# A second MLP in two passes, with both of its products made of seven block products

## The chip, the cores and the metric

The kernel runs on one core of a Trainium2 chip, with all five engines of that core: TensorE (PE) for matmuls, VectorE (DVE), ScalarE (ACT) and GpSimd (POOL) for the rest, SyncE (SP) for most DMAs. The metric is the time of one execution on the device, in microseconds.

## The reference

All is float32. Three parts follow one another on 4 batches of 576 tokens and 512 features:

```python
x  = attention(q, k, v)                    # 8 heads of 64; half local, half strided masks
u  = x + real(fft(fft(x, axis=1), axis=2)) # 4 x 576 x 512
x  = u + relu(norm(u) @ w_ch1) @ w_ch2     # first MLP, 512 -> 2048 -> 512
h  = relu(x.T @ w_tok1) @ w_tok2           # token mixing, 576 -> 256 -> 576
u  = x + h.T
out = u + relu(u @ w_ch1b) @ w_ch2b        # second MLP, 512 -> 1536 -> 512
```

Each float32 operand of a product is kept as a high and a low part in a format that PE takes, and a product is three matmuls: high by high, high by low, low by high.

## The kernel before

PE's work lies in this order: attention with the Fourier part, the first MLP (class Mlp, L381 and L399, six chunks of 384 tokens by 16 blocks f of hidden features), the token mixing (c1 at L704, c2 at L724, batch by batch), and the second MLP. A scheduler sets the order of the instructions on each engine from the order of the program and its dependencies; tile pools decide when a buffer may be written again.

The second MLP takes 9 chunks of 256 tokens. A chunk has 6 steps m. In each, gemm1 makes two blocks of h, for features f = m + 6 and m, with 24 matmuls of 256 columns (L777); ACT takes them out of PSUM with the relu (L783, L784), DVE forms four sums of 128-column blocks (L789) and the low parts (L791, L792), ACT the high part of the sums (L790); gemm2 multiplies 2 by 2 blocks of h by 2 by 2 blocks of w2b with seven block products in place of eight, each of three matmuls of 256 columns, 21 matmuls a step (L807). At a chunk's end eleven additions on DVE (L831) combine the seven products into the result, which is stored.

The seven combinations of w2b are made ahead: blocks() is called 12 times, at f % 4 == 1 of the first MLP's chunks 2 to 4. It loads raw weights in double precision, turns them into float32 on ACT and DVE (L92 to L97), adds blocks on POOL (L120), splits them into high and low on ACT and POOL (L123, L124), and SP stores them to DRAM (wsd). POOL's queue loads them again in 42 DMAs (L619). The 12 blocks of w1b are converted in the last chunk of the first MLP (load_wb). Results of the token mixing go to DRAM (u2d, L735), come back in tiles of 128 tokens (u_load, L753) and are transposed on PE (L762).

## Time and profile before

| | us |
|---|---|
| three runs | 950.62, 954.13, 953.64 (median 953.64) |
| span of the profiled execution | 947.8 |
| between the span and the median | 5.8 |
| PE busy in the span | 919.9 (97%) |
| DVE, ACT, POOL busy | 538.8, 374.1, 205.2 |

The profile gives one execution's span, from the first to the last instruction; no other time of that execution is given, and the runs are timed from outside. A busy time counts a matmul up to its modelled end, so that matmuls overlap: the distance between the starts of two of them is what PE needs for one. Idle time of an engine that nobody waits for costs nothing.

### The profile page before, as it was taken

Reading aid. Unit: us, or ns where it says so; the run is one execution under the profiler, and the core shown is the slowest. Engines: PE = TensorE matmul, PEld = TensorE weight load, DVE = VectorE, ACT = ScalarE, POOL = GpSimd, SP = SyncE. Lnnn points to the kernel's source line nnn. Section 1 sums busy time; section 2 is a strip of 40 time slices with the busy share of each in tenths; the row PEclk is TensorE's granted clock in tenths of the full one; section 3 lists DMA queues with packets and bytes.
Section 4 is the critical chain, followed back from the end, with each engine's and each line's share of the span. In section 5 each row is a group of like instructions: output and inputs, shape, how many; then the busy total and the mean of one; then the engine's idle time right before and its main releaser. Section 6 shows DMA issues by size and latency. Waiting matters only on the chain.

```text
span 947.8 us, 16036 instructions
## 1 busy us (share of the span) xinstructions
PE 919.9 (97%) x6094; PEld 850.5 (90%) x6094; DVE 538.8 (57%) x1182; ACT 374.1 (39%) x998; POOL 205.2 (22%) x230
## 2 busy tenths in 40 slices
PE   6979999999999999999999999999999999999997
PEld 5969998899888888999999988779999999999997
DVE  4659987898975544321213678444545545553554
ACT  5969776444433334121112445212333333333332
POOL 4213203233344354000000666342000000000000
PEclk9979999999999999999999999999999999999999
DMA  9988862344436767200100445598011101100000
GB/s 261 275 273 258 264 199 88 105 157 142 152 105 212 235 187 206 90 1 1 67 1 5 150 147 161 159 288 269 12 34 45 42 5 46 46 24 22 24 24 23
DMA packets 73286, 113.85 MB, mean 120 GB/s; under 512 B 6803, under 2 KB 39417, under 8 KB 73209
## 3 DMA queue, kind: packets, MB, share of 16 engines
q1 hardware_dynamic: 65192, 99.09, 33.4%
q0 software_dynamic: 7760, 13.52, 5.0%
q8 instruction: 48, 0.79, 0.4%
q10 hardware_dynamic: 256, 0.21, 0.1%
q14 instruction: 30, 0.24, 0.1%
HBM read 78.97 MB, written 33.82 MB: 119 GB/s over the span
## 4 chain that ended last, share of the span: by engine, by line
PE 71%; DVE 9%; DMA 7%; issue 5%; ACT 3%; POOL 3%; SPq 1%; DVEq 0%; POOLq 0%; ACTq 0%
PE h L777 16%; PE oo L807 14%; PE oo L399 12%; PE h L381 12%; PE tk L704 3%; PE tu L724 3%; PE sc L180 2%; DMA wraw<-in_w2a_dram 2%; PE av L222 2%; DVE wu L96 2%; DMA wraw<-in_w2b_dram 1%; DVE wu L97 1%; PE g L302 1%; DVE wu L94 1%; DMA wsd<-wbl 1%
## 5 line engine op out<-in xcount | busy, mean ns | idle before, releaser
L807 PE MATMUL oo<-w2b,hh 128*128 128x256 f32 x756 | 140.4, 284 | 0.0
L381 PE MATMUL h<-uth,wAh 128*128 128x384 f32 x384 | 130.2, 340 | 0.0
L381 PE MATMUL h<-utl,wAh 128*128 128x384 f32 x384 | 129.6, 337 | 0.0
L381 PE MATMUL h<-uth,wAl 128*128 128x384 f32 x384 | 129.5, 337 | 0.0
L777 PE MATMUL h<-uth,w1bl 128*128 128x256 f32 x432 | 120.9, 280 | 0.0
L777 PE MATMUL h<-utl,w1bh 128*128 128x256 f32 x432 | 120.8, 280 | 0.0
L386 DVE SCALAR_TENSOR_TENSOR hl<-h,hh 128x384 fp32r<-128x384 f32 x96 | 53.1, 553 | 119.0 <-ACT hh L385 119.0
L777 PE MATMUL h<-uth,w1bh 128*128 128x256 f32 x432 | 120.7, 280 | 0.0
L399 PE MATMUL oo<-wAh,hh 128*128 128x512 f32 x288 | 114.5, 399 | 2.9 <-ACT hh L385 1.6
L807 PEld LDWEIGHTS oo<-w2b,hh 128*128 128x128 f32 x756 | 116.2, 189 | 0.0
L399 PE MATMUL oo<-wAl,hh 128*128 128x512 f32 x288 | 113.6, 395 | 0.0
L399 PE MATMUL oo<-wAh,hl 128*128 128x512 f32 x288 | 106.1, 397 | 1.4 <-DVE hl L386 1.3
L807 PE MATMUL oo<-w2b,hl 128*128 128x256 f32 x378 | 104.4, 282 | 0.0
L385 ACT ACTIVATE hh<-h 128x384 fp32r<-128x384 f32 x96 | 46.1, 483 | 118.1 <-PE h L381 117.9
L789 DVE TENSOR_TENSOR hz<-hw 128x128 f32<-128x128 f32 x108 | 26.6, 287 | 114.0 <-ACT hw L783 114.0
L783 ACT ACTIVATE hw<-h 128x512 f32<-128x512 f32 x54 | 32.3, 599 | 148.4 <-PE h L777 148.4
L777 PEld LDWEIGHTS h<-uth,w1bh 128*128 128x128 f32 x432 | 81.3, 188 | 0.2
L777 PEld LDWEIGHTS h<-uth,w1bl 128*128 128x128 f32 x432 | 81.2, 188 | 0.1
L777 PEld LDWEIGHTS h<-utl,w1bh 128*128 128x128 f32 x432 | 81.2, 188 | 0.1
L381 PEld LDWEIGHTS h<-uth,wAl 128*128 128x128 f32 x384 | 72.2, 188 | 3.0
L381 PEld LDWEIGHTS h<-utl,wAh 128*128 128x128 f32 x384 | 72.2, 188 | 2.9
L381 PEld LDWEIGHTS h<-uth,wAh 128*128 128x128 f32 x384 | 72.1, 188 | 2.0
(166 smaller groups left out, 1866.1 us busy)
## 6 DMA issues: line engine op xcount, KB each, us to landing
w2b<-wsd POOLq DMA_DIRECT2D x42, 256.0 KB, 5.3
wraw<-in_w1a_dram SPq DMA_DIRECT2D x16, 512.0 KB
wraw<-in_w2a_dram SPq DMA_DIRECT2D x16, 512.0 KB
wraw<-in_w2b_dram SPq DMA_DIRECT2D x48, 128.0 KB
wraw<-in_w1b_dram SPq DMA_DIRECT2D x12, 512.0 KB
wsd<-wbh SPq DMA_DIRECT2D x12, 448.0 KB
wsd<-wbl SPq DMA_DIRECT2D x12, 448.0 KB
out_dram<-u SPq DMA_DIRECT2D x16, 256.0 KB
```

The costliest lines, as they stand in the source:

```text
L96: v.scalar_tensor_tensor(out=u, in0=high, scalar=-2**31, in1=u, op0=ALU.bitwise_and, op1=ALU.bitwise_or)
L180: last = nc.tensor.matmul(out=sc[:q, j * k:(j + 1) * k], lhsT=qz[self.g][:, e, hp, qs], rhs=k_t[self.b, self.g][:, hp, ks], start=False, s ...
L381: nc.tensor.matmul(out=h[:, :384], lhsT=l[:, ws], rhs=r[:, kd, :], start=x == 0, stop=x == 11)
L385: nc.scalar.activation(out=hh, in_=h[:, :384], func=AF.Relu)
L386: nc.vector.scalar_tensor_tensor(out=hl, in0=h[:, :384], scalar=0.0, in1=f32(hh), op0=ALU.max, op1=ALU.subtract)
L399: nc.tensor.matmul(out=self.o[c][i], lhsT=l[:, s], rhs=r, start=first and x == 0, stop=last and x == 2)
L704: nc.tensor.matmul(out=hp[m], lhsT=wt1(w, t, m)[q], rhs=r[q], start=t == 0 and x == 0, stop=t == 4 and x == 2)
L724: nc.tensor.matmul(out=o[:q0 + n], lhsT=wt2(w, k, 128 * t - q0, q0 + n), rhs=r, start=k == 0 and x == 0, stop=k == 1 and x == 2)
L777: nc.tensor.matmul(out=h[:, 256 * i:256 * i + 256], lhsT=l[:, ws], rhs=r[:, kd, 0:256], start=x == 0, stop=x == 11)
L783: nc.scalar.activation(out=w, in_=h, func=AF.Relu)
L789: nc.vector.tensor_tensor(out=o, in0=x, in1=y, op=op)
L807: ends.append(nc.tensor.matmul(out=acc[c][bank][:, 256 * half:256 * half + 256], lhsT=lh[:, s], rhs=r, start=m == 0 and x == 0 and half == ...
```

## The change

The first product of the second MLP is now made of seven block products as well, and the second MLP goes in two passes. Tokens are taken in three superchunks of 768. u_stage loads and transposes six tiles of a superchunk; u_ops forms the block sums and splits the seven operands. A Unit is one step m of a superchunk: seven products, each of six matmuls of 384 columns (L821). The sums build up in three PSUM banks z, y and w; ACT copies z at three points (snap), DVE adds the copies into h (into), and relu stands at the end (ACT for one block, DVE for three). Units go in pairs, their products interleaved by hand (double). The h of the first two superchunks goes to DRAM (hd) and is loaded again; that of the last stays in SBUF.

The second pass has its order written out by hand: 54 steps of 21 matmuls of 256 columns, as before, over 9 groups G of 256 tokens. In it h is loaded six steps ahead and split three steps ahead (h_split: the four sums now on POOL, two copies on ACT, two subtractions on DVE), and finish() combines the products; for the last group bank by bank. blocks() is called 24 times, for w1b too, and load_wb's conversions of w1b are gone. All block operands are loaded on SP's queue (load_ops). The low parts of the token mixing's input for batches 2 and 3 move from DVE to POOL.

```diff
...
-NP2, NC2 = NF2 // 2, 9
+NP2, NS = NF2 // 2, 3
...
-    def blocks(m, c0):
...
+    def blocks(w, m, c0):
+        src = a["w" + w + "b"]
+        order = ((0, 256), (0, 0), (1, 0), (1, 256)) if w == "2" else ((1, 0), (0, 0), (0, 256), (1, 256))
...
-        for o, x, y in ((t1, b12, b11), (t2, b22, t1), (t3, b22, b12), (t4, t2, b21)):
-            nc.gpsimd.tensor_tensor(out=o, in0=x, in1=y, op=ALU.subtract)
...
+        for o, x, y, plus in sums:
+            nc.gpsimd.tensor_tensor(out=o, in0=x, in1=y, op=ALU.add if plus else ALU.subtract)
...
-            nc.sync.dma_start(out=wsd[m][:, :, o:o + 128].rearrange("b p c -> p b c"),
+            nc.sync.dma_start(out=wsd[w][m][:, :, o:o + 128].rearrange("b p c -> p b c"),
...
-            elif len(w1b) < NF2:
-                f = len(w1b)
-                pool, tag = (wa, "wa") if f < 2 else (wb, "wb") if f < 10 else (wc, "wc")
-                w1b.append(slot_w(a["w1b"][f], pool, tag, "w1b"))
-
-        def load_w2(ms):
...
-                    nc.gpsimd.dma_start(out=t, in_=wsd[m][x])
...
+        def load_ops(w, m):
+            wo[w, m] = []
...
+                nc.sync.dma_start(out=f32(t), in_=wsd[w][m][x])
+                wo[w, m].append(t)
...
-                nc.vector.tensor_tensor(out=l[q], in0=r[q], in1=f32(h[q]), op=ALU.subtract)
+                (nc.gpsimd if b > 1 else nc.vector).tensor_tensor(out=l[q], in0=r[q], in1=f32(h[q]), op=ALU.subtract)
...
-                blocks(m, 128 * h)
+                blocks("2", m, 128 * h)
+            if 2 <= c < NCH - 1 and f % 4 == 3:
+                m, h = divmod((c - 2) * 4 + f // 4, 2)
+                blocks("1", m, 128 * h)
...
-                if b == 0 and t < 3:
-                    u2[t] = r
-                else:
-                    nc.sync.dma_start(out=u2d[p][j, q, :], in_=r[q])
+                nc.sync.dma_start(out=u2d[p][j, q, :], in_=r[q])
...
-        def gemm1(c, m):
...
+        def u_stage(s):
+            q = [ga.tile([P, 4, 384], F32, tag=nm, name=nm, bufs=1) for nm in ("qa", "qb")]
...
+                for half in range(2):
+                    u = u_load(6 * s + 3 * half + i)
+                    tp = ps_m("ut")
+                    for kd in range(4):
+                        nc.tensor.transpose(tp[:, kd * P:(kd + 1) * P], u[:, kd * P:(kd + 1) * P], ident)
+                    nc.scalar.activation(out=q[half][:, :, i * P:(i + 1) * P],
+                                         in_=tp.rearrange("p (k t) -> p k t", k=4), func=AF.Copy)
+            return q
+
+        def u_ops(s, q):
+            qa, qb = q
...
+            eng = nc.vector if s == 0 else nc.gpsimd
+            for o, x, y, e in ((t1, b12, b11, eng), (t2, b22, t1, eng), (b12, b22, b12, nc.gpsimd), (t4, b21, t2, nc.gpsimd)):
+                e.tensor_tensor(out=o, in0=x, in1=y, op=ALU.subtract)
+            src = dict(b11=b11, b21=b21, t2=t2, t1=t1, t3=b12, t4=t4, b22=b22)
+            U[s] = {}
+            for nm in UB:
+                t = gp.tile([P, 12, P], F32R, tag=nm, name="u" + nm, bufs=1)
+                h, l = (t[:, c:c + 6].rearrange("p (k g) t -> p k (g t)", k=2) for c in (0, 6))
+                nc.scalar.activation(out=h, in_=src[nm], func=AF.Copy)
+                e = nc.gpsimd if s == 0 and nm in ("t3", "b22") else nc.vector
+                e.tensor_tensor(out=l, in0=src[nm], in1=f32(h), op=ALU.subtract)
+                U[s][nm] = h, l
...
+            def product(self, n, bank, first):
+                i, nm = PRODUCTS[n]
+                w = wo["1", self.m][i]
+                h, l = U[self.s][nm]
                 x = 0
-                for kd in range(4):
-                    ws = slice(kd * P, (kd + 1) * P)
-                    for l, r in ((wh, th), (wh, tl), (wl, th)):
-                        nc.tensor.matmul(out=h[:, 256 * i:256 * i + 256], lhsT=l[:, ws], rhs=r[:, kd, 0:256],
-                                         start=x == 0, stop=x == 11)
+                for kd in range(2):
+                    for c, r in ((0, h), (0, l), (256, h)):
+                        Unit.last = nc.tensor.matmul(out=bank[:, :384], lhsT=w[:, c + kd * P:c + kd * P + P], rhs=r[:, kd],
+                                         start=first and x == 0, stop=x == 5,
+                                         skip_group_check=True)
...
+            def snap(self):
+                t = wa.tile([P, 512], F32, tag="wa", name="snap")[:, :384]
+                nc.scalar.activation(out=t, in_=self.z[:, :384], func=AF.Copy)
+                return t
...
+            def into(self, i, bank, t):
+                for o, x, y in self.pieces(i, bank, t):
+                    nc.vector.tensor_tensor(out=o, in0=x, in1=y, op=ALU.add)
+
+            def step(self, n):
+                if n == 1:
+                    self.z = ps_h("z")
+                    self.product(1, self.z, True)
+                    self.q1 = self.snap()
+                elif n == 2:
+                    w = ps_o("w")
+                    self.product(2, w, True)
+                    self.into(2, w, self.q1)
+                elif n == 6:
+                    self.product(6, self.z, False)
+                    self.u1 = self.snap()
+                elif n == 5:
+                    self.y = ps_o("y")
+                    self.product(5, self.y, True)
+                    if self.u2 is not None:
+                        self.into(1, self.y, self.u2)
+                elif n == 7:
+                    self.product(7, self.z, False)
+                    self.u2 = self.snap()
+                    if self.y is not None:
+                        self.into(1, self.y, self.u2)
+                elif n == 4:
+                    self.product(4, self.z, False)
+                    for o, x in self.pieces(0, self.z):
+                        nc.scalar.activation(out=o, in_=x, func=AF.Relu)
+                elif n == 3:
+                    self.product(3, self.y, False)
+                    self.into(3, self.y, self.u1)
+
+            def store(self):
+                for p in self.parts:
+                    nc.vector.tensor_scalar_max(p[:, :, 1:4], p[:, :, 1:4], 0.0)
+                    if self.s < NS - 1:
+                        nc.sync.dma_start(out=hd[self.s][self.m], in_=p.rearrange("p g i t -> p (g i t)"))
+
+        def double(s, m, then={}):
+            a, b = Unit(s, m), Unit(s, m + 1)
+            for x, n in ((a, 1), (b, 1), (a, 2), (b, 2), (a, 6), (b, 6), (a, 5), (a, 7), (b, 7), (b, 5),
+                         (a, 3), (b, 3), (a, 4), (b, 4)):
+                x.step(n)
+                if x is a and n == 4:
+                    a.store()
+                if x is b and n in then:
+                    h_split(*then[n])
+            b.store()
...
         c_load(3, range(5))
-        for b in range(2, 4):
-            hs.append(c1(b))
-        for T in range(2):
-            transposes(T)
-        for b in range(2, 4):
-            c2(b, hs[b])
-        load_w2(range(1, NP2))
-
...
-        steps = [(c, m) for c in range(NC2) for m in range(NP2)]
-        for i, (c, m) in enumerate(steps):
-            gemm1(c, m)
-            if c + 1 < NC2:
...
+        hs.append(c1(2))
+        load_ops("1", 0)
+        c2(2, hs[2])
+        q = u_stage(0)
+        load_ops("1", 1)
+        u_ops(0, q)
+        hs.append(c1(3))
+        c2(3, hs[3])
+        for m in range(2, NP2):
+            load_ops("1", m)
...
+        Gs = [3 * NS - 3, 3 * NS - 2, 3 * NS - 1] + list(range(3 * NS - 3))
+        steps = [(G, m) for h in ((0, 4), (4, NP2)) for G in Gs[:2] for m in range(*h)]
+        steps += [(G, m) for G in Gs[2:] for m in range(NP2)]
...
+        def h_load(G, m):
+            s, g = divmod(G, 3)
+            if s < NS - 1:
+                if m % 3 == 0:
+                    h_load.t = ha.tile([P, 3, 4, P], F32, tag="hs", name="hw", bufs=3)
+                w = rows[G, m] = h_load.t[:, m % 3]
+                nc.sync.dma_start(out=w, in_=hd[s][m][:, 512 * g:512 * g + 512].rearrange("p (i t) -> p i t", i=4))
...
+        def h_split(G, m):
+            w = rows.pop((G, m))
+            z = wa.tile([P, 4, P], F32, tag="wa", name="hz")
+            a12, a22, a11, a21 = (w[:, i] for i in range(4))
+            s1, s2, s3, s4 = (z[:, i] for i in range(4))
+            t = gp.tile([P, 12, P], F32R, tag=UB[steps.index((G, m)) % NP2], name="ht", bufs=1)
+            wh, wl, zh = (t[:, c:c + n] for c, n in ((0, 3), (3, 3), (6, 4)))
+            zl = wa.tile([P, 4, P], F32R, tag="wa", name="zl")
+            nc.scalar.activation(out=wh, in_=w[:, 0:3], func=AF.Copy)
+            for o, x, y, op in ((s1, a21, a22, ALU.add), (s2, s1, a11, ALU.subtract), (s3, a11, a21, ALU.subtract),
+                                (s4, a12, s2, ALU.subtract)):
+                nc.gpsimd.tensor_tensor(out=o, in0=x, in1=y, op=op)
+            nc.vector.tensor_tensor(out=wl, in0=w[:, 0:3], in1=f32(wh), op=ALU.subtract)
+            nc.scalar.activation(out=zh, in_=z, func=AF.Copy)
+            nc.vector.tensor_tensor(out=zl, in0=z, in1=f32(zh), op=ALU.subtract)
+            ops[G, m] = wh, wl, zh, zl
+
+        for s in range(NS):
+            if s + 1 == NS:
+                gast.close()
+                ha = hst.enter_context(tc.tile_pool(name="ha", bufs=1, side="left", reuse_waits="tile"))
+            for m in range(0, NP2, 2):
+                double(s, m, {2: steps[0], 6: steps[1], 5: steps[2]} if s + 1 == NS and m == NP2 - 2 else {})
+                if m == 0 and s + 1 < NS:
+                    q = u_stage(s + 1)
+                if s + 1 == NS:
+                    load_ops("2", m)
+                    load_ops("2", m + 1)
+            if s + 1 < NS:
+                u_ops(s + 1, q)
+
+        BANKS = ((0, 0, "w", 2, 0), (0, 1, "z", 1, 4), (1, 0, "z", 2, 5), (1, 1, "z", 0, 3), (2, 0, "w", 0, 1),
...
+
+            def fourth():
+                v(c21, c21, o[3][:, 0:256], ALU.subtract)
...
+            if G != Gs[-1]:
+                gemm2(G, [NP2 - 1], BANKS)
+            for bank, part in enumerate((first, second, third, fourth)):
+                if G == Gs[-1]:
+                    gemm2(G, [NP2 - 2, NP2 - 1], BANKS[2 * bank:2 * bank + 2])
+                part()
+            acc.pop(G)
+            return store
...
+        ahead, split, later, us2 = 6, 3, {}, {}
+        with tc.manual_schedule():
+            for x, (G, m) in enumerate(steps):
                 if m == 0:
-                    for T in (2 * c + 2, 2 * c + 3):
-                        if T > 2:
-                            u_load(T)
-                if m in (2, 3):
-                    transposes(2 * c + m)
-            if i:
-                gemm2(*steps[i - 1])
-        gemm2(*steps[-1])
+                    acc[G] = [(ps_o if Gs.index(G) % 2 else ps_h)("oo") for _ in range(3)] + [ps_m("oo")]
+                    us2[G] = u_load(6 * (G // 3) + G % 3), u_load(6 * (G // 3) + G % 3 + 3)
+                if x in later:
+                    later.pop(x)()
+                if x + ahead < len(steps):
+                    h_load(*steps[x + ahead])
+                if x + split < len(steps):
+                    h_split(*steps[x + split])
+                if m == NP2 - 1:
+                    later[x + 3] = finish(G)
+                elif G != Gs[-1] or m < NP2 - 2:
+                    gemm2(G, [m], BANKS)
+            for x in later:
+                later[x]()
```

Up to the first new block sums, in chunk 2 of the first MLP, the instructions stand in the same order in both kernels. Three places behind that show what is moved.

PE where the second MLP begins, before (tu: token mixing, h: the first product) and then after (ut: transposes, z: a first-product bank):

```order
L724 MATMUL tu<-uth,wth 128x512
L724 MATMUL tu<-utl,wth 128x512
L724 MATMUL tu<-uth,wtl 128x512
L777 MATMUL h<-uth,w1bh 128x256 x2
L777 MATMUL h<-utl,w1bh 128x256
L777 MATMUL h<-uth,w1bl 128x256
L777 MATMUL h<-uth,w1bh 128x256
L777 MATMUL h<-utl,w1bh 128x256
```

```order
L732 MATMUL tu<-hl,wth 128x512
L732 MATMUL tu<-hh,wtl 128x512
L732 MATMUL tu<-hl,wth 128x512
L732 MATMUL tu<-hh,wtl 128x512
L821 MATMUL z<-ub_6645,wo 128x384 x12
L732 MATMUL tu<-hh,wth 128x512 x3
L769 MATMUL ut<-ident_r,u 128x128 x4
L732 MATMUL tu<-hl,wth 128x512
```

Before, the first product starts between the last batch's matmuls with 256 columns; now products of 384 columns stand between matmuls of the mixing, in sixes and twelves.

SP in the same place, before and then after (wo: the block operands; cr and x2d: inputs of the mixing; u2d: its results; u: tiles loaded for the transposes):

```order
L653 DMA cr<-x2d_78 128x512 x3
L735 DMA u2d_79<-u 128x512
L735 DMA u2d_79<-u 64x512
L753 DMA u<-u2d_79 128x512
L735 DMA u2d_79<-cr 128x512 x3
L653 DMA cr<-x2d_78 64x512
L735 DMA u2d_79<-cr 128x512
L735 DMA u2d_79<-cr 64x512
L753 DMA u<-u2d_79 128x512 x2
```

```order
L622 DMA wo<-wsd_84 128x512
L740 DMA u2d_79<-u 128x512 x3
L756 DMA u<-u2d_79 128x512
L622 DMA wo<-wsd_82 128x512 x5
L740 DMA u2d_79<-u 128x512
L740 DMA u2d_79<-u 64x512
L622 DMA wo<-wsd_83 128x512
L756 DMA u<-u2d_79 128x512
L740 DMA u2d_79<-cr 128x512
L756 DMA u<-u2d_79 128x512
L622 DMA wo<-wsd_83 128x512 x2
L740 DMA u2d_79<-cr 128x512 x2
```

Before, SP had only the mixing's loads and stores and the tiles here, since POOL's queue loaded the block operands; now the operands stand between stores and tiles in one queue.

DVE in the second MLP's steps before, then DVE after (ht and zl: low parts; lm and u: combining the products), then POOL after (hz: sums of blocks of h):

```order
L792 TENSOR_TENSOR hl<-hz,hh 128x512
L789 TENSOR_TENSOR hz<-hw 128x128 x2
L789 TENSOR_TENSOR hz<-hz,hw 128x128
L791 TENSOR_TENSOR hl<-hw,hh 128x384
L789 TENSOR_TENSOR hz<-hw,hz 128x128
L766 TENSOR_TENSOR utl<-ut,uth 128x4x128
```

```order
L929 TENSOR_TENSOR ht<-hw,ht 128x384
L931 TENSOR_TENSOR zl<-hz,ht 128x512
L973 TENSOR_TENSOR lm<-oo,lm 128x256 x2
L973 TENSOR_TENSOR u<-oo,u 128x256 x2
L973 TENSOR_TENSOR u<-u,lm 128x512
L973 TENSOR_TENSOR u<-oo,u 128x512
L973 TENSOR_TENSOR u<-u,lm 128x512
L973 TENSOR_TENSOR u<-u,oo 128x256
L929 TENSOR_TENSOR ht<-hw,ht 128x384
L931 TENSOR_TENSOR zl<-hz,ht 128x512
```

```order
L928 TENSOR_TENSOR hz<-hw 128x128
L928 TENSOR_TENSOR hz<-hw,hz 128x128
L928 TENSOR_TENSOR hz<-hw 128x128
L928 TENSOR_TENSOR hz<-hz,hw 128x128
L928 TENSOR_TENSOR hz<-hw 128x128
```

The four additions of 128 columns have left DVE, where they stood between the low parts, and POOL, which had none in this stage, has them one after another.

## Rows read from the trace of the kernel before

**Rows 1.** The page, part 2: tenths of busy time in 40 slices.

```profile
PE   6979999999999999999999999999999999999997
...
PEclk9979999999999999999999999999999999999999
```

**Rows 2.** Stretches: length, busy time of each engine (instructions), granted clock, DMA share, GB/s.

```profile
250.00:400.00 150.00, 147.40 (x732) 129.67 (x732) 85.86 (x161) 51.24 (x100) 59.98 (x80) 1.00 0.57 174
...
600.00:650.00 50.00, 50.00 (x226) 37.88 (x225) 21.26 (x32) 7.61 (x14) 20.28 (x36) 1.00 0.83 255
650.00:941.00 291.00, 291.00 (x2464) 290.99 (x2462) 150.37 (x431) 96.89 (x186) 1.33 (x3) 1.00 0.11 35
941.00:948.00 7.00, 0.20 (x2) 0.00 (x0) 3.06 (x9) 0.00 (x0) 0.00 (x0) 0.79 0.19 75
```

**Rows 3.** Groups of instructions from 640 us on: busy us, mean ns, idle before.

```profile
L807 PE MATMUL oo<-w2b,hh 128*128 128x256 f32 x756 | 140.4, 284 | 0.0
L777 PE MATMUL h<-uth,w1bl 128*128 128x256 f32 x432 | 120.9, 280 | 0.0
...
L792 DVE TENSOR_TENSOR hl<-hz,hh 128x512 fp32r<-128x512 f32 x54 | 37.3, 691 | 26.2 <-ACT hh L790 26.1
...
L791 DVE TENSOR_TENSOR hl<-hw,hh 128x384 fp32r<-128x384 f32 x54 | 29.7, 550 | 0.0
```

**Rows 4.** Timeline of PE, second MLP: start us, us, engine, line and operation.

```profile
699.74 0.28 PE L777 MATMUL h<-uth,w1bl 128*128 128x256 f32 x1
...
701.50 0.28 PE L777 MATMUL h<-uth,w1bl 128*128 128x256 f32 x1
```

**Rows 5.** Timeline of PE, first MLP, products of 384 columns.

```profile
420.87 0.34 PE L381 MATMUL h<-uth,wAh 128*128 128x384 f32 x1
...
423.35 0.34 PE L381 MATMUL h<-uth,wAl 128*128 128x384 f32 x1
```

**Rows 6.** The chain of waits at the end: start us, us, what.

```profile
930.85 2.52 PE oo L807 x21
...
936.19 3.47 PE oo L807 x29
...
943.76 0.34 DVE u L831
```

**Rows 7.** Timeline of SP at the end.

```profile
943.79 0.81 SPq L834 DMA_DIRECT2D out_dram<-u  x2
```

**Rows 8.** Timeline of SP: raw loads of the first and the fourth of four block sets.

```profile
334.87 2.08 SPq L88 DMA_DIRECT2D wraw<-in_w2b_dram  x4
...
358.17 1.77 SPq L88 DMA_DIRECT2D wraw<-in_w2b_dram  x4
```

**Rows 9.** Groups of POOL over the whole span.

```profile
L120 POOL TENSOR_TENSOR wt<-wu 128x128 f32<-128x128 f32 x24 | 10.6, 462 | 39.8 <-DVE wu L97 39.8
```

**Rows 10.** Timelines of POOL and DVE near 270 us and 543 us, where both work.

```profile
270.17 0.69 DVE L96 SCALAR_TENSOR_TENSOR wu<-wraw,wu 128x512 int32<-128x512 int32 x1
270.90 1.67 DVE L97 SCALAR_TENSOR_TENSOR wu<-wraw,wu 128x512 int32<-128x512 int32 x1
...
270.54 1.47 POOL L103 TENSOR_TENSOR wAl<-wu,wAh 128x512 fp32r<-128x512 f32 x1 [3.25 <-ACT wAh L102]
...
543.71 1.33 POOL L103 TENSOR_TENSOR w1bl<-wu,w1bh 128x512 fp32r<-128x512 f32 x1 [1.94 <-ACT w1bh L102]
...
543.82 1.78 DVE L96 SCALAR_TENSOR_TENSOR wu<-wraw,wu 128x512 int32<-128x512 int32 x1
```

**Rows 11.** Timeline of POOL: additions of 128 columns back to back.

```profile
289.33 0.88 POOL L120 TENSOR_TENSOR wt<-wu 128x128 f32<-128x128 f32 x2 [4.36 <-DVE wu L97]
290.17 0.46 POOL L120 TENSOR_TENSOR wt<-wu,wt 128x128 f32<-128x128 f32 x1
```

**Rows 12.** Stretches around a long wait of PE, columns as in rows 2.

```profile
57.00:64.00 7.00, 0.29 (x3) 0.15 (x2) 4.18 (x13) 1.88 (x7) 1.59 (x2) 0.79 1.00 344
64.00:71.00 7.00, 6.95 (x31) 6.18 (x32) 4.96 (x11) 6.04 (x26) 1.47 (x2) 0.50 0.90 273
```

More of the change, by code (lines that the diff above doesn't have):

```diff
@@ new lines, in u_load @@
+            u = lp.tile([P, DM], F32, tag="u", name="u", bufs=6)
+            nc.sync.dma_start(out=u, in_=u2d[T // 9][T % 9])
+            return u
+        U = {}
+        UB = ("b11", "b21", "t2", "t1", "t3", "t4", "b22")
+        def u_stage(s):
+            q = [ga.tile([P, 4, 384], F32, tag=nm, name=nm, bufs=1) for nm in ("qa", "qb")]
+            for i in range(3):
+                for half in range(2):
[6 more added lines that the diff above has]
+            return q
@@ L867, in attention_fourier_mlp_kernel @@
+        gst.close()
+        hst.close()
         wcst.close()
```

216 lines of the change are left out of this document (115 added, 101 removed).

## The prediction

> **What bounds the kernel now.** I read four views, in this order: the slices, the stretches, the groups of instructions, and last the chain of waits. The slices show PE at 9 from the fifth slice to the last but one, at the granted clock's upper level nearly throughout [rows 1]. The stretches make that sharp: from 650 to 941 us PE is busy 291.0 of 291.0 us and DVE 150.4, with POOL at 1.3 and the DMA share at 0.11 [rows 2]. So the second MLP is bound by the number of matmul columns on PE; DVE has half its time free, POOL all of it. The chain ends in the same way: PE alone up to 939.66 us, then some 4 us of DVE, then the stores [rows 6]. Hence I price first what the change takes off PE, and after that everything that could stop PE from running without gaps.
>
> **The change part by part.**
>
> *First product of the second MLP.* Before: 3 x 432 = 1,296 matmuls of 256 columns at L777 [rows 3]. One issues every (701.50 - 699.74)/15 = 0.1173 us [rows 4]: the group's 280 ns is the time of one in the pipeline, not its price. Sum 152.0 us. After: 3 superchunks x 6 steps x 7 products x 6 matmuls = 756 of 384 columns at L821. The first MLP has such matmuls, one every (423.35 - 420.87)/14 = 0.1771 us [rows 5], sum 133.9 us. Difference: **-18.1 us**. It is all on the path, as PE has no gap there. The second product keeps its 1,134 matmuls of 256 columns, and the transposes stay 72.
>
> *Tail.* Before, the last matmul ends near 941.1 and the span at 947.8 us: 6.7 us for the additions at L831, of which the last ends at 944.1, and stores issued at 943.79 [rows 6, 7]; the second issue ends at 944.60, 3.2 us before the end. After, the last tile's banks are added one by one while PE still works, so behind the last matmul stand one addition of 256 columns, one issue and the landing: 0.4 + 0.4 + 3.2 = 4.0, and I allow 0.3 for hand-overs. **-2.4 us**, bounds -3 and +1 (the copies of the banks, on ACT, come late).
>
> *Twelve more sets of block sums.* Twelve sets for w1b join twelve for w2b during chunks 2 to 4 of the first MLP. A set's loads come every (358.17 - 334.87)/3 = 7.8 us [rows 8], so 24 sets take some 187 us from 261 on, to about 450, well before the token mixing, which holds the stretch from 600 on [rows 2]. ACT and DVE serve PE between them; the stretch that held the twelve lost PE 150 - 147.4 = 2.6 us [rows 2]. As many again would be +2.6; what the twelve conversions of w1b that go had cost is not counted. I take **+1.5**, bounds 0 and 6 (twice the loss seen, and the first sets delay one another).
>
> *Into the second MLP.* All tiles now make the round trip through DRAM, six are transposed, and DVE and POOL form seven operands for 768 tokens before the first product; SP's queue carries 42 operand loads between them, which were POOL's. Queued behind a waiting SP load are the u2d stores and the next batch's loads, and for those PE waits. The cover is the token mixing of the last two batches, whose matmuls stand between the products in PE's new order. That cover shares the DMA engines with the loads: 0.83 busy at 255 GB/s in that stretch [rows 2], and 14 operand loads of 256 KB are needed for the first pair, 3.7 MB or 14 us at that rate. I follow the chain by hand through the order and find 0 to 2 us of slack at two operands. Estimate **+3**, bounds 0 and 10.
>
> *Between the products.* Sums build up in three kinds of PSUM bank with copies between; the tight place is product 3, which waits for an addition (0.55 us for 384 columns [rows 3]) behind product 5 with one product of the other step, 6 x 0.1771 = 1.06 us, between. That fits unless DVE is in another instruction. There are nine pairs and three starts of a superchunk: **+2**, bounds 0 and 9 (a microsecond in each pair).
>
> *Second product: POOL beside DVE.* This is the term with the widest bounds. Each of 54 steps is 21 matmuls, 2.52 us of PE [rows 6], and needs four additions of 128 columns, now on POOL, and two subtractions (384 and 512 columns) on DVE, all with two inputs in SBUF. The trace of before shows that such instructions do not run together. A DVE instruction of 512 columns that took 0.69 us alone took 1.67 and 1.78 beside a POOL instruction, each ending 0.56 us after POOL's end (272.57 against 272.01; 545.60 against 545.04). And where DVE was first, POOL's 512 columns took 1.47 us and ended 1.15 after DVE's end (272.01 against 270.86) [rows 10]. So one shuts the other out for most of its time: 0.56 of 0.69 on DVE, about 0.13 less than its duration, and on POOL about 0.15 less than an undisturbed one. For POOL's 128 columns at 0.462 [rows 9] that leaves 0.31; for DVE's 384 columns at 0.55 [rows 3], 0.42.
>
> Per step, the exclusive part is 4 x 0.31 + 0.56 + 0.42, and a sixth of two 512-column additions of each finished tile, 0.19: 2.41 us, below the 2.52 of PE. But POOL's own starts are 0.42 apart ((290.17 - 289.33)/2 [rows 11]), and a DVE instruction that slips in holds it up for its exclusive part less the 0.11 that is free anyway: 4 x 0.42 + 1.17 - 2.33 x 0.11 = 2.59 us per step. The lower bound of the cost is nothing (2.41 fits). If nothing slips into POOL's gaps, a step is 1.68 + 1.17 = 2.85 us and the cost 0.33 x 51 = 17 us; at the far end, with whole durations one after another, it is 4 x 0.462 + 0.55 + 0.69 + 2 x 0.69 / 6 = 3.32 us, and 0.80 x 51 = 41 us. I take POOL's 2.59, as rows 10 and 11 are nearest to it: (2.59 - 2.52) x 51 = 3.6, and with the waits of the first steps **+5**.
>
> The Trainium skill has a rule for this, in "SBUF — State Buffer", section "Who interferes with whom": a DVE instruction with two SBUF inputs contends with a POOL instruction that reads SBUF, and whichever was first has the ports for its whole instruction. Rows 10 agree on the blocking and show a shorter hold. Taken at its word it speaks against the change, by the far end above; by the rows it costs 5.
>
> *Round trip of h.* Twelve stores of 768 KB in 90 us of products, and 36 loads of 256 KB over as many steps, beside a DMA share of 0.11 [rows 2]: covered, issued six steps ahead. If a load were late, PE would wait once, not in every step.
>
> **The sum.** The profiled execution has a span of 947.8 us; the median of the runs is 953.64, so 5.8 lie outside the span, by the median, and I leave them as they are. 953.6 - 18.1 - 2.4 + 1.5 + 3 + 2 + 5 = **944.6**, I say 945.
>
> **The rivals.**
>
> A. *The port decides the second product, and the change loses.* POOL and DVE exclude each other, and neither slips into the other's gaps. For it: rows 10, and that PE can't start a step without both engines' results. Against: the exclusive parts add to 2.41, and POOL may run three steps ahead. The point from which it makes the kernel slower than before is a step of 2.52 + (5 + 9)/51 = 2.79 us, since my forecast with its 5 has 9 in hand. At 2.85 the time is 939.6 + 17 = 957, at whole durations 939.6 + 41 = 981. I give it 957 to 981, mostly the lower half.
>
> B. *A long wait at the entry.* If the first operands come 7 us late, PE idles and the clock falls as well: after the long wait at 57 to 64 us the next 7 us ran at 0.50 of full clock, the lower level of 1.2 GHz [rows 12], which costs another 3.5 or so. 944.6 - 3 + 10.5 = 952, within half a per cent. For it: 0.83 DMA share [rows 2]. Against: the token mixing of the last batches is there to fill.
>
> C. *The gain goes into the products' gaps.* The copies and additions of each pair stop PE by a microsecond or more per pair, and block sums cost their 6: 944.6 + 7 + 4.5 = 956, about no change. Against: DVE has half its time free [rows 2].
>
> D. *Nothing is late*: no port cost, entry covered, 953.6 - 18.1 - 2.4 = 933. For it: 291.0 of 291.0 busy before [rows 2], with DVE half loaded.
>
> **How the numbers follow.** Half a per cent, 4.8 us, is about what a measurement of this kernel can tell from no change. My forecast 0.45 (own range 938 to 950: nearly all faster), D 0.14 (faster), B 0.10 and C 0.12 (mostly the same), A 0.19 (slower). The forecast leaves 0.03 for the same. Faster: 0.42 + 0.14 + 0.02 = 0.58; same 0.22; slower 0.20. The range from 934 to 963 leaves out part of D and the upper half of A.
>
> **What would show it.** PE from the first to the last product of 384 columns in about 134 us, without gaps over 1 us, and a granted clock of 1.00 there, show the first term. A step of 21 matmuls in the second product of 2.52 us means that the port costs nothing; of 2.6, my term; of 2.8 or more, with PE waiting for DVE's subtraction or POOL's addition, rival A. DVE's 512-column subtractions well above 0.69 us in that stage show the exclusion; at 0.69 with POOL busy beside them they would refute it. A clock under 1.00 at 600 to 660 us shows B. The forecast is wrong if PE idles over 10 us in all within the second MLP.

## The result, and the profile after

The changed kernel takes 941.16 us in the median of four runs (937.12 to 945.76), the kernel before 952.35 beside it: a ratio of 0.9894, 95% interval 0.9853 to 0.9936. The forecast was 945, with 934 to 963 as its range. Its profiled execution has a span of 938.2 us and took 940.05.

Of the page's slices, in tenths, PE's are the same as in [rows 1]; POOL's and the granted clock's are

```profile
...
POOL 3312302233345355544430411303213013999995
PEclk9889999999999999999999999999999999999999
```

The stretches of the changed kernel, with the columns of [rows 2]:

```profile
250.00:400.00 150.00, 144.92 (x719) 127.29 (x718) 88.15 (x166) 54.95 (x106) 68.57 (x97) 1.00 0.61 188
400.00:520.00 120.00, 117.95 (x601) 105.67 (x600) 44.67 (x86) 35.96 (x69) 39.66 (x56) 1.00 0.48 145
...
600.00:650.00 50.00, 50.00 (x222) 37.24 (x221) 18.23 (x26) 12.45 (x21) 6.29 (x5) 1.00 0.71 232
650.00:790.00 140.00, 138.06 (x798) 136.34 (x797) 69.70 (x97) 54.25 (x105) 28.88 (x24) 1.00 0.57 198
790.00:930.00 140.00, 137.52 (x1133) 135.87 (x1132) 113.17 (x178) 57.97 (x117) 132.13 (x204) 1.00 0.40 132
...
```

PE is still dense, but no longer everywhere: from 250 to 520 us, in the first MLP, it misses 7.1 of 270 us, where the kernel before missed 2.6 up to 400 us. The last 140 us before 930 are new: POOL is busy for 132.1 of 140 us, and PE misses 2.5. What PE waits for, from 200 us on (sum in us, times, longest):

```profile
PE oo L407 <- ACT hh L393: 4.9, 6, 1.2
PE oo L407 <- DVE hl L394: 1.8, 3, 0.8
PE z L821 <- DVE ut L789: 1.7, 1, 1.7
PE oo L958 <- DVE ht L929: 1.5, 4, 0.4
PE oo L958 <- DVE zl L931: 1.2, 5, 0.2
```

These waits of PE add up to 11.1 us: 6.7 in the first MLP (7.0 with the few of other causes), 1.7 at the entry into the second, 2.7 in the second product. In the kernel before, PE waits in the first MLP for 3.1 us (0.2 of them for another cause) and nowhere behind it:

```profile
PE oo L399 <- ACT hh L385: 1.6, 3, 1.0
PE oo L399 <- DVE hl L386: 1.3, 3, 0.7
```

Three groups that work on h in the second product of the changed kernel:

```profile
L928 POOL TENSOR_TENSOR hz<-hw 128x128 f32<-128x128 f32 x72 | 55.2, 767 | 0.0
...
L931 DVE TENSOR_TENSOR zl<-hz,ht 128x512 fp32r<-128x512 f32 x54 | 47.2, 873 | 23.9 <-ACT ht L930 23.9
...
L929 DVE TENSOR_TENSOR ht<-hw,ht 128x384 fp32r<-128x384 f32 x36 | 27.4, 762 | 0.0
```

The two DVE groups answer to the rows of L791 and L792 in [rows 3]: 0.55 us became 0.76, 0.69 became 0.87. POOL's addition of 128 columns, 0.462 us in [rows 9], takes 0.77 in its largest group.

Where the spans' difference of 9.6 us comes from, read from the timelines of both executions at four marks:

| stretch, by its marks | before | after | difference |
|---|---|---|---|
| start to the last store of the Fourier part | 215.8 | 217.3 | +1.6 |
| from there to the last matmul of the first MLP | 373.1 | 377.5 | +4.5 |
| first matmul of the token mixing to the last matmul of all | 359.4 | 345.1 | -14.3 |
| end of the last matmul to the end of the span | 6.6 | 5.3 | -1.3 |

The first line is not the change's: the order of instructions is the same there in both kernels. The granted clock accounts for it: in the changed kernel's execution, stretches of 17.4 us in all before 217 us ran at 0.51 to 0.52, in the other's 14.0 us at 0.51; 3.4 us more at half the clock are 1.7 us. Between the second and third marks both kernels go on without a gap in time. (The third stretch starts 7 us before the second ends, in both alike.)

### The profile page after: what moved, and what is told of

Read it like the earlier page. It is cut to its first block, busy times and chain, and to the rows that moved or that the text cites. A ratio compares the mean times of both kernels' runs of the same rounds, so it can differ in the third digit from the quotient of the medians.

```text
span 938.2 us, 15514 instructions
## 1 busy us (share of the span) xinstructions
PE 903.0 (96%) x5554; PEld 830.4 (89%) x5554; DVE 560.8 (60%) x1024; ACT 400.3 (43%) x1053; POOL 366.4 (39%) x474
## 4 chain that ended last, share of the span: by engine, by line
PE 48%; POOL 13%; DVE 12%; DMA 12%; issue 8%; ACT 4%; SPq 3%; DVEq 0%; POOLq 0%; ACTq 0%
POOL hz L928 10%; PE h L389 8%; PE oo L407 8%; PE z L821 8%; PE y L821 4%; PE tk L710 3%; PE tu L732 3%; DMA wraw<-in_w2a_dram 2%; PE sc L188 2%; DVE wu L97 2%; DMA wraw<-in_w2b_dram 2%; PE av L230 2%; PE w L821 2%; DMA wraw<-in_w1b_dram 2%; PE g L310 2%
## 5 line engine op out<-in xcount | busy, mean ns | idle before, releaser
L958 PE MATMUL oo<-wo,ht 128*128 128x256 f32 x918 | 135.8, 281 | 1.5 <-DVE ht L929 1.5
L958 PEld LDWEIGHTS oo<-wo,ht 128*128 128x128 f32 x918 | 124.7, 189 | 2.3 <-DVE ht L929 2.3
L394 DVE SCALAR_TENSOR_TENSOR hl<-h,hh 128x384 fp32r<-128x384 f32 x96 | 52.9, 553 | 93.6 <-ACT hh L393 93.6
L104 POOL TENSOR_TENSOR wAl<-wu,wAh 128x512 fp32r<-128x512 f32 x32 | 43.7, 1371 | 86.4 <-ACT wAh L103 77.9
L407 PEld LDWEIGHTS oo<-wAh,hh 128*128 128x128 f32 x288 | 54.1, 188 | 17.5 <-ACT hh L393 7.1
L407 PEld LDWEIGHTS oo<-wAh,hl 128*128 128x128 f32 x288 | 53.4, 188 | 16.4 <-DVE hl L394 4.5
L930 ACT ACTIVATE ht<-hz 128x512 fp32r<-128x512 f32 x54 | 34.1, 632 | 77.9 <-POOL hz L928 77.9
L821 PE MATMUL z<-ut,wo 128*128 128x384 f32 x324 | 64.5, 339 | 1.7 <-DVE ut L789 1.7
L93 ACT ACTIVATE wu<-wraw 128x512 f32<-128x512 f32 (+1 forms) x62 | 41.4, 668 | 57.6 <-POOL wAl L104 18.4
L958 PE MATMUL oo<-wo,zl 128*128 128x256 f32 x216 | 61.2, 283 | 1.2 <-DVE zl L931 1.2
L407 PEld LDWEIGHTS oo<-wAl,hh 128*128 128x128 f32 x288 | 54.1, 188 | 8.6
```

What stands on the lines that cost most here:

```text
L93: nc.scalar.activation(out=f32(u), in_=f32(high), func=AF.Abs, scale=2.0**16)
L104: nc.gpsimd.tensor_tensor(out=lo, in0=f32(u), in1=f32(hi), op=ALU.subtract)
L394: nc.vector.scalar_tensor_tensor(out=hl, in0=h[:, :384], scalar=0.0, in1=f32(hh), op0=ALU.max, op1=ALU.subtract)
L407: nc.tensor.matmul(out=self.o[c][i], lhsT=l[:, s], rhs=r, start=first and x == 0, stop=last and x == 2)
L821: Unit.last = nc.tensor.matmul(out=bank[:, :384], lhsT=w[:, c + kd * P:c + kd * P + P], rhs=r[:, kd], start=first and x == 0, stop=x == 5, ...
L930: nc.scalar.activation(out=zh, in_=z, func=AF.Copy)
```

## Experiments

Two marks of the table are used throughout: "the first MLP's stage" is its second line, "mixing to end" its third. They tell more than the runs' times, since the stages before 217 us vary: their end lay between 214.7 and 220.7 us in these traces, with one order. "Mixing to end" hardly varies: in the changed kernel and the five runs that leave these matmuls as they are (e1_no_w1_sets, e8_no_w1_sets_b, e7_copies, e10_staged_alone, e4_whole_tail) it was 345.1 to 345.2 us. The times were taken in several sessions, in which the kernel before had medians of 950.4 to 952.6 us; so differences of some 2 us between times of different sessions show nothing.

**Is it the shared port?** The theory is that POOL's additions and DVE's subtractions shut each other out ("the port" is the prediction's word for it; the traces show the exclusion, not what causes it). The changed kernel's timelines at 861 us show it as alternation (DVE and POOL; start, duration):

```profile
861.12 0.81 DVE L929 TENSOR_TENSOR ht<-hw,ht 128x384 fp32r<-128x384 f32 x1
...
861.48 0.78 POOL L928 TENSOR_TENSOR hz<-hw,hz 128x128 f32<-128x128 f32 x1
...
861.86 0.95 DVE L931 TENSOR_TENSOR zl<-hz,ht 128x512 fp32r<-128x512 f32 x1
...
862.22 0.90 POOL L928 TENSOR_TENSOR hz<-hw 128x128 f32<-128x128 f32 x1
...
862.73 0.81 DVE L929 TENSOR_TENSOR ht<-hw,ht 128x384 fp32r<-128x384 f32 x1
```

POOL's first one ends 0.33 us after DVE's (862.26 against 861.93), DVE's next one, of 512 columns, 0.55 after POOL's (862.81), POOL's 0.31 after that (863.12), DVE's of 384 columns 0.42 after (863.54). Those are the exclusive parts that the prediction worked out: 0.31 us for POOL's, 0.56 and 0.42 for DVE's.

PE's waits name DVE, but POOL stands behind them. From 850 to 930 us ACT waits for POOL's sums, and DVE, with its subtractions in one queue, for ACT; POOL itself waits for nothing there:

```profile
ACT ht L930 <- POOL hz L928: 45.8, 29, 2.3
DVE zl L931 <- ACT ht L930: 15.3, 15, 1.0
```

*Without DVE's part (e2_no_low):*

```diff
...
-            nc.vector.tensor_tensor(out=wl, in0=w[:, 0:3], in1=f32(wh), op=ALU.subtract)
             nc.scalar.activation(out=zh, in_=z, func=AF.Copy)
-            nc.vector.tensor_tensor(out=zl, in0=z, in1=f32(zh), op=ALU.subtract)
-            ops[G, m] = wh, wl, zh, zl
+            ops[G, m] = wh, wh, zh, zh
```

> This kernel leaves out the low parts of h in the second product (DVE's two subtractions per step; the matmuls stay 21 a step, with the high part read twice), so its time is read for the pace alone. Theory P (POOL's additions are stretched from 0.46 us to 0.54-0.77 by DVE's two-input subtractions): without them POOL's 128-column additions go back to 0.46-0.50 us on average, POOL's busy time in the last 140 us falls from 132 to about 100, PE's nine short waits there (2.7 us in all) go, and the time falls by 2 to 4 us. Rival Q (POOL is slowed by the DMA traffic of h or by its own queue): the additions stay above 0.6 us and the time within 1 us.

Measured: no wait of PE in the second product, mixing to end 341.8 us against 345.1. The median was 941.57 us; in this execution the first MLP's stage was 2.6 us longer and the stages before it 3.4, which hides the 3.3 in the time. The groups of POOL and the stretch, of this kernel:

```profile
L927 POOL TENSOR_TENSOR hz<-hw 128x128 f32<-128x128 f32 x72 | 35.1, 488 | 31.1 <-DMA hw<-hd 27.5 <-ACT ht L928 3.7
...
L927 POOL TENSOR_TENSOR hz<-hw,hz 128x128 f32<-128x128 f32 x36 | 18.1, 502 | 0.0
```

```profile
790.00:930.00 140.00, 140.00 (x1144) 140.00 (x1143) 36.09 (x79) 59.78 (x123) 93.83 (x206) 1.00 0.42 142
```

POOL's additions are back at 0.49 to 0.50 us, its busy time at 93.8, and PE has no gap in 140 us. Theory P is shown: DVE's subtractions are what stretches POOL's additions. The DMA traffic of h was the same here, so Q falls. The gain in the whole time was not seen.

*One addition more (e5_five):*

```diff
                 nc.gpsimd.tensor_tensor(out=o, in0=x, in1=y, op=op)
+                if o is s3:
+                    nc.gpsimd.tensor_tensor(out=o, in0=x, in1=y, op=op)
```

> One of POOL's four additions per step is done twice, five in all. Theory P, POOL's queue at the edge: a step goes from about 2.69 us of POOL to 2.69 + 0.42 to 0.55 = 3.1 to 3.25, against 2.5 of PE, so 54 steps cost 54 x 0.65 less the 7 us of lead: +22 to +33 us on the time. Rival Q' (POOL has slack that the trace doesn't show, the waits come from DVE's or ACT's order): +0 to +6 us.

Measured: 965.22 us, ratio to the kernel before 1.014 (1.0087 to 1.0193), mixing to end 367.6 us against 345.1. Two of PE's waits, six steps apart, in this kernel and then in the changed one:

```profile
874.14 0.63 PE L960 MATMUL oo<-wo,ht 128*128 128x256 f32 x3 [1.56 <-DVE ht L931]
...
892.90 0.50 PE L960 MATMUL oo<-wo,ht 128*128 128x256 f32 x2 [1.97 <-DVE ht L931]
```

```profile
892.65 0.63 PE L958 MATMUL oo<-wo,ht 128*128 128x256 f32 x3 [0.42 <-DVE ht L929]
...
908.78 0.62 PE L958 MATMUL oo<-wo,ht 128*128 128x256 f32 x3 [0.43 <-DVE ht L929]
```

A step is (892.90 - 874.14)/6 = 3.13 us with five additions, and (908.78 - 892.65)/6 = 2.69 with four. One more addition is 0.44 us of every step, and the time is 24 us longer: POOL's queue had no slack left. In the changed kernel PE waits this way only from 876 us on, apart from one wait of 0.2 us at 788; in between, what POOL had done ahead covers it.

*The sums back on DVE (e3_sums_dve):*

```diff
-                nc.gpsimd.tensor_tensor(out=o, in0=x, in1=y, op=op)
+                nc.vector.tensor_tensor(out=o, in0=x, in1=y, op=op)
```

> The four sums of h's blocks go back to DVE, as in the kernel before; POOL has nothing in the second product. Theory P: no exclusion, DVE's subtractions return to 0.55 and 0.69 us, but DVE then has 1.93 + 4 x 0.24 to 0.29 = 2.9 to 3.1 us a step against 2.5 of PE: +20 to +30 us. Rival Q (the exclusion costs so much that moving the sums was a loss): the same or faster than the changed kernel.

Measured: 957.05 us, ratio 1.0062 (1.0040 to 1.0083): slower than the kernel before. PE's waits, six steps apart, in this kernel:

```profile
885.62 0.58 PE L958 MATMUL oo<-wo,ht 128*128 128x256 f32 x2 [1.96 <-DVE ht L929]
...
903.34 0.58 PE L958 MATMUL oo<-wo,ht 128*128 128x256 f32 x2 [1.95 <-DVE ht L929]
```

(903.34 - 885.62)/6 = 2.95 us a step. DVE is busy for 54.0 of the 60 us from 870 us on, and its subtractions are back at 0.55 and 0.69 us, as expected. PE waits long once in six steps, where the additions that combine a group (3.9 us on DVE from 880.31) stand ahead of the next step's parts. The 16 us over the changed kernel (16.8 from mixing to end, 361.9 against 345.1) are fewer than the 20 to 30 expected: DVE, like POOL, had a lead at the start, and PE's first long wait ends at 832 us. So POOL's part is worth its place even with the exclusion.

*One of the four sums on DVE (e6_three):*

```diff
-                nc.gpsimd.tensor_tensor(out=o, in0=x, in1=y, op=op)
+                (nc.vector if o is s3 else nc.gpsimd).tensor_tensor(out=o, in0=x, in1=y, op=op)
```

> One of POOL's four sums per step (s3) goes to DVE. Theory P (POOL's queue is at the edge, DVE has room): POOL's step falls from 2.69 to about 2.2 us, DVE's rises from about 2.06 to 2.35 to 2.45, both under 2.5 of PE: PE's waits of 2.7 us in the second product fall below 1, from the mixing's first matmul to the last one 342 to 343 us against 345.1, and the time falls by 2 to 3 us. Rival (DVE becomes the edge): waits of 2 us or more, the same time.

Measured: 941.36 us, mixing to end 344.0; PE's waits in the second product are down from 2.7 us to

```profile
PE oo L958 <- DVE zl L931: 0.7, 3, 0.2
```

The stage gained 1.0 us of the 2 to 3 expected, more than it varies without a change; no difference can be seen in the time.

**What do the block sets cost?** Six of these kernels have the changed kernel's code up to the second product; their first MLP's stage was 376.2 to 380.1 us, 377.5 in the changed kernel itself, each read from one execution. The changed kernel's ACT, from 250 to 450 us, waits for (sum, times, longest):

```profile
ACT wbh L131 <- DVE wu L98: 44.5, 19, 3.0
ACT wbh L131 <- POOL wt L128: 34.4, 19, 2.4
...
ACT wu L93 <- DMA wraw<-in_w2b_dram: 8.1, 10, 2.4
...
ACT wu L93 <- DMA wraw<-in_w1b_dram: 6.2, 7, 1.7
```

*Without the sets of w1b, first try (e1_no_w1_sets):* each store of a set of w2b stands twice, the calls for w1b are gone.

```diff
+            for k in "21":
-                nc.sync.dma_start(out=wsd[w][m][:, :, o:o + 128].rearrange("b p c -> p b c"),
+                nc.sync.dma_start(out=wsd[k][m][:, :, o:o + 128].rearrange("b p c -> p b c"),
...
-            if 2 <= c < NCH - 1 and f % 4 == 3:
-                m, h = divmod((c - 2) * 4 + f // 4, 2)
-                blocks("1", m, 128 * h)
```

> This kernel leaves out the twelve block sets of w1b (their loads, conversions, sums and splits in the first MLP); the sets of w2b are stored twice in their place, so the second MLP's work is unchanged. Theory B (the sets cost 4.4 us: ACT's copies for them stand ahead of the first MLP's own): PE's waits from 250 to 520 us fall from 7.0 to about 3 us and the first MLP ends 4 to 5 us earlier. Rival B' (the later end comes from the earlier stages and from loads, not from the sets): it ends within 1 us of the changed kernel's 594.8, less what the stages up to 250 us differ.

Measured: the opposite, 947.40 us, the stage 384.0. The second stores, which had been taken as free, stand in SP's queue ahead of a set's last raw load. SP and ACT near 298 us, and two stretches of this kernel:

```profile
291.42 2.03 SPq L135 DMA_DIRECT2D wsd<-wbl  x2
293.50 1.29 SPq L89 DMA_DIRECT2D wraw<-in_w2b_dram  x1
...
297.93 0.66 ACT L93 ACTIVATE wu<-wraw 128x512 f32<-128x512 f32 x1 [10.17 <-DMA wraw<-in_w2b_dram]
...
299.45 0.88 ACT L394 ACTIVATE hh<-h 128x384 fp32r<-128x384 f32 x2
```

```profile
290.00:300.00 10.00, 7.33 (x40) 6.56 (x38) 1.25 (x3) 2.07 (x5) 0.00 (x0) 1.00 0.76 221
300.00:310.00 10.00, 10.00 (x44) 8.82 (x45) 8.09 (x16) 3.50 (x7) 3.97 (x6) 0.83 0.59 186
```

ACT stood 10.2 us for a raw load, with the first MLP's copy (hh, L394) queued behind, and PE ran dry: 7.33 busy in 10 us. In the next 10 us the granted clock was 0.83. The run says nothing on the number of sets, but shows how a set can stop PE.

*Second try, without the second stores (e8_no_w1_sets_b):*

```diff
...
-                nc.sync.dma_start(out=f32(t), in_=wsd[w][m][x])
+                nc.sync.dma_start(out=f32(t), in_=wsd["2"][m][x])
...
-                blocks("1", m, 128 * h)
```

> As e1_no_w1_sets, without its second stores: the twelve sets of w1b are left out, and the first product's operands are read from w2b's places in DRAM, so it computes with other weights. From the last store of the Fourier part to the last matmul of the first MLP the kernel before took 373.1 us, the changed one 377.5 (376.2 and 380.1 in two runs with the same order there), e1 384.0. Theory B'' (ACT stands still, with the first MLP's own copies queued behind, whenever a set's data are late; fewer sets, fewer such waits; e1's second stores made its raw loads late): 372 to 375 us, PE's waits in it 3 to 4 us. Rival (the later end has nothing to do with the sets): 377 us or more.

Measured: 935.18 us, the stage 372.7 us; the kernel before has 373.1. PE's waits in this kernel's first MLP:

```profile
PE oo L407 <- ACT hh L393: 1.9, 3, 1.0
...
PE oo L407 <- DVE hl L394: 0.9, 2, 0.6
...
```

So the twelve sets cost 377.5 - 372.7 = 4.8 us of the stage (3.5 to 7.4 by the spread of the runs with one order). Leaving them out takes work off ACT, DVE, POOL and SP's queue at once; which of these costs the time is not shown by it.

*Can that be had back?* Three edits took set copies out of ACT's way: both off ACT, both ordered later, or one to DVE. Both off ACT (e7_copies):

```diff
-            nc.scalar.activation(out=hi[:, s], in_=x, func=AF.Copy)
+            (nc.gpsimd if x is t else nc.vector).tensor_copy(out=hi[:, s], in_=x)
```

> The two copies to the high part in each block set leave ACT: the first goes to DVE, behind the instruction that it waits for, the second to POOL, behind the additions. Theory B'': ACT no longer waits for DVE's and POOL's parts of a set (79 us of waits at L131 in the changed kernel), so PE's 7.0 us of waits in the first MLP fall to 2 to 4, that stage from 377.5 to 373 to 375 us, and the time by 2 to 4 us, to 937 to 939. Rival (the waits come from the loads, or POOL's longer set makes the chain the bound): stage 377 us or more, time 941 or above.

Measured: 939.94 us, the stage 378.1, PE's waits there 7.1 us, no fewer than before. ACT, from 250 to 450 us, now waits for

```profile
ACT wu L93 <- DMA wraw<-in_w2b_dram: 38.8, 8, 7.4
ACT wu L93 <- DMA wraw<-in_w1b_dram: 36.1, 8, 6.5
```

75 us for raw loads in place of 79 for DVE and POOL. With the sets staged over three blocks, alone (e10_staged_alone) and with s3 of the second product on DVE (e9_staged):

```diff
...
+            behind(nc.scalar.activation(out=hi[:, s], in_=x, func=AF.Copy), Mlp.last)
...
+        due.extend([second, third])
...
+            if due:
+                due.pop(0)()
```

> The changed kernel with each block set cut in three: loads, conversion and DVE's part at its old place, the sums and the first copy one block f later, the second copy and the stores another f later, each copy ordered behind that block's own copy of the first MLP on ACT. Theory B'' (the sets cost 4.8 us because ACT stands waiting for a set's data with the first MLP's copy behind it): the copies now come some 4 us after what they need, PE's waits in the first MLP fall from 7.0 to 3 or 4 us, that stage from 377.5 to 373 to 375 us, the time to 936.5 to 939. Rival (a set's cost is in its loads, as the run with the copies on DVE and POOL left open): the stage stays at 377 or more, the time at 941.

> The same with s3 of the second product on DVE, as in e6_three, which took 1.0 us off the stage from the mixing's first matmul to the last (344.0 against 345.1). If the two add up: 935.5 to 938, about 1.6% under the kernel before. If only the staging works 936.5 to 939, if neither, 941.

Measured: 944.81 and 943.99 us, the stage 382.0 and 379.1. From mixing to end the second took 343.7 us, so s3 on DVE gave its 1 us or more again. ACT's waits from 250 to 520 us in the first of the two:

```profile
ACT wu L93 <- DMA wraw<-in_w2b_dram: 34.3, 10, 6.2
...
ACT wbh L130 <- DVE wu L98: 27.3, 12, 2.8
ACT wu L93 <- DMA wraw<-in_w1b_dram: 27.0, 10, 5.2
...
```

One copy to DVE (e11_one_copy), on top of an edit of the second MLP that follows under the tail (e12_six_tail) and leaves the first MLP as it is:

```diff
...
-            nc.scalar.activation(out=hi[:, s], in_=x, func=AF.Copy)
+            if x is t:
+                nc.scalar.activation(out=hi[:, s], in_=x, func=AF.Copy)
+            else:
+                nc.vector.tensor_copy(out=hi[:, s], in_=x)
```

> As e12_six_tail, and the first of the two copies of a block set goes from ACT to DVE, behind the instruction that makes its input; the second stays on ACT. Theory B'' (ACT's waits in the sets' order): ACT's waits for DVE at the first copy (52 us) go without a new early wait for loads, the first MLP's stage falls from 377.5 to 374 to 376 us, the time to 937 to 938. Rival (as in e7_copies and e10_staged_alone, another part of the set makes ACT wait in its place): stage 377 us or more, the time as e12_six_tail's.

Measured: 947.71 us, the stage 381.3; ACT, from 250 to 520 us:

```profile
ACT wbh L132 <- POOL wt L128: 96.9, 24, 5.7
```

In all of them another part of the same chain (load, ACT, DVE, POOL, ACT, POOL, store) makes ACT wait in its place, with the copies of the first MLP behind, and the stage is no shorter than the 376.2 to 380.1 us of the runs with the changed kernel's order. That the sets cost time through ACT's order agrees with this, but no run sets that order apart from the work itself; and none shows a way to place twelve more sets there at less.

**The tail.** In the changed kernel, the last matmuls, DVE's last three additions and SP's stores:

```profile
932.04 0.87 PE L958 MATMUL oo<-wo,ht 128*128 128x256 f32 x6
...
933.06 0.68 DVE L973 TENSOR_TENSOR u<-oo,u 128x512 f32<-128x512 f32 x1
933.17 2.14 SPq L1007 DMA_DIRECT2D out_dram<-u  x3
933.78 0.69 DVE L973 TENSOR_TENSOR u<-u,lm 128x512 f32<-128x512 f32 x1
934.38 0.41 DVE L973 TENSOR_TENSOR u<-u,oo 128x256 f32<-128x256 f32 x1
```

The last group finished like the others (e4_whole_tail; the same edit at each place that asks for the last group):

```diff
-                if G == Gs[-1]:
+                if G == -1:
...
```

> The last group is finished like the others: all matmuls first, then the additions on DVE, then two stores. Theory T (the bank by bank finish is worth the time that DVE works behind the last matmul): from the end of the last matmul to the span's end 6.5 to 7.5 us instead of 5.3, and the time 1 to 2 us up. Rival (the stores' landing alone sets the end): 5.3 us as before.

Measured: 944.08 us; 6.3 us from the last matmul's end to the span's end, against 5.3. The bank by bank finish is worth 1.0 us, a little less than expected. Moving one addition ahead of the third bank, with s3 on DVE (e12_six_tail):

```diff
...
+                v(ua, ua, w)
             def third():
                 v(ua, o[2], ua)
-                v(ua, ua, w)
```

> The changed kernel with s3 on DVE (as e6_three) and with one addition of the finish moved ahead: w is added to ua before the third bank is complete, so one 512-column instruction fewer stands on DVE behind the last matmul. If the tail is DVE's work plus the landing: from the end of the last matmul to the span's end 4.6 to 4.8 us against 5.3, and with e6_three's 1.0 us the time 1.5 to 2 us under the changed kernel's (about 939.5). Rival (the stores' issues on SP set the end): 5.3 us, only e6_three's gain.

Measured: 944.88 us; the tail 5.3 us as before, and PE's waits in the second product 3.5 us instead of 0.7. That the moved addition does nothing at the end can be read from the changed kernel: DVE works there without a break from 931.44 us, when it gets the second bank's copy, to 934.79, and the third bank is complete before DVE comes to it; so the addition only changes places in a full queue. In every group it has two inputs in SBUF, and from mixing to end it took more than e6_three's gain away (347.7 us here, 347.3 in e11_one_copy, against 344.0); why, is not settled.

No version that does all of the work beats the changed kernel by more than these runs can tell.

## Why the prediction was right, step by step

*What bounds the kernel, and the first product (-18.1).* Right. Mixing to end fell by 14.3 us; with the 1.7 and 2.7 of waits taken out, by 18.7 against 18.1. The run without DVE's part gives 17.6, or 19.3 without the entry's 1.7. The half to one us more is in the matmuls' distances: by their starts, the first product took 133.3 us without its one wait (reckoned: 133.9), and 152.2 before (152.0); and in the run without DVE's part the second product's matmuls stood 120.0 ns apart, against 120.7 before, 0.8 us in all.

*Tail (-2.4).* Right in its direction, wrong in its size: 6.6 became 5.3. The term put one addition behind the last matmul, as if DVE kept up with the banks. But DVE is behind from the second bank on, and when the matmuls end, at 932.9 us, the third bank's two additions of 512 columns still stand ahead of the last one: 1.9 us of work in all.

*Twelve more sets (+1.5).* The most mis-sized term: 4.8 us, inside its bounds of 0 and 6. The step had +2.6 by the number of sets and took 1.5, with no number for the twelve conversions that go. These are worth little: without w1b's sets, and without the conversions, the stage is 372.7 us, with the conversions before 373.1. PE waited 3.1 us in this MLP with twelve sets (3.0 in e8_no_w1_sets_b), and 7.0 with 24 (5.6 to 8.6 in the runs with the same order): the second twelve cost about as much again as the first, or more. ACT's waits from 250 to 450 us for PE's products, before and then after, show what was left out:

```profile
ACT hh L385 <- PE h L381: 51.8, 17, 5.0
```

```profile
ACT hh L393 <- PE h L389: 0.6, 1, 0.6
```

Before, ACT had 51.8 us in which it stood ready for PE's next product; after, it stood ready only once, for 0.6 us: by the time that ACT comes to a product, past the sets' copies and the waits ahead of them, it is finished. That slack is what the term left out.

*Into the second MLP (+3).* One wait of 1.7 us, for an operand's low part on DVE (L789), and not the 3 us allowed. Rival B did not come: the clock was 1.00 from 600 to 790 us.

*Between the products (+2).* Nothing: apart from that one wait PE has none in the first product. Rival C falls.

*POOL beside DVE (+5).* The mechanism was right, and the exclusive parts to 0.02 us. The step of POOL was forecast at 2.59 us and is 2.69; the cost was forecast at 5 us and is 2.7 by PE's waits, 3.3 by the run without DVE's part, since POOL's lead lasts until 876 us and only some 20 of the 54 steps run at POOL's pace. The Trainium skill's rule ("SBUF — State Buffer", "Who interferes with whom") says that two such instructions contend, and the trace agrees: 0.77 us in place of 0.46 for POOL's addition. The same section speaks of an exclusive lock, and in its line on DVE's two-port modes of a hold for the whole instruction; carried over to these instructions, as the prediction did, that would be 3.32 us a step, far from the 2.69 measured. Rival A did not come; its point of 2.79 us a step, from which the change loses, agrees with the run with five additions, which loses at 3.13 (965.22). Rival D falls with the 4.4 us for which PE waits in the second MLP.

*The sum.* 944.6 against 941.16: the terms for the gaps, the entry and the port were 5.6 too high together, those for the sets and the tail 4.4 too low, and 952.35 stands for the kernel before where 953.64 was taken. That the total comes within 3.4 us is luck in part: the main mechanisms held, but five of the terms were off by 1.1 to 3.3 us, and the errors mostly cancel.

## What to carry to other kernels

Count work that two engines share a port for by its exclusive part: take it from the trace as the time from one engine's end to the other's, add it up per step with the engine's own gaps, and compare the sum with the pace of the engine that bounds the kernel. The sum is a floor: here the exclusive parts gave 2.41 us, with POOL's gaps 2.59, and 2.69 was measured. An engine a little too slow is hidden for as many steps as its lead lasts. Preparatory work that is placed beside a dense stage can cost that stage through the order of the queue that both use: look at what stands behind each instruction that waits, and at how much slack is left in that queue; the loss seen, scaled by the number of pieces, was too little here (2.6 against 4.8). When several terms of both signs make up a forecast, read each from its own stage afterwards; the total can be right with single terms off by 2 or 3 us.

## What the runs showed of the hardware

A wait of PE can cost more than its length, since the granted clock can fall to its lower level behind it; but the length alone does not decide whether it does. In the first run without w1b's sets, the 10 us after a wait of 2.7 us had a granted clock of 0.83, and so had the stretch from 430 to 440 us of the same run, around a wait of 1.6 us. With the sums on DVE, two waits of 1.96 and 1.95 us, which ended at 885.62 and 903.34 us, were followed by 10 us at 1.00 and at 0.83. With both set copies off ACT, the wait of

```profile
408.66 0.50 PE L407 MATMUL oo<-wAh,hh 128*128 128x512 f32 x1 [2.24 <-ACT hh L393]
```

was followed by 10 us at 1.00, as were the waits of up to 1.7 us in the changed kernel's second MLP. What decides it is left open by these runs.
